# One quarter of a weight matrix on a second DMA queue, a denser request schedule and two reordered places, in a kernel of windowed attention and soft mixture of experts

## The chip, the cores and the metric

The kernel runs on one core of one Trainium2 chip. A core has a matrix engine (PE, with its weight loads shown apart as PEld), a vector engine (DVE), an activation engine (ACT), a general engine (POOL), a sync engine (SP) that only issues and waits, and sixteen DMA engines that move data between device memory and the on-chip memory. The metric is the device time of one execution in microseconds, the median over several runs.

## The reference

Eight batches of eight heads, 576 positions, 64 values a head. Each position attends to a window behind it: heads 0 to 3 to the last 32 positions, heads 4 to 7 to every fourth of the last 128. The result, 4608 rows of 512, goes through a soft mixture of experts: the rows are mixed into 32 slots (4 for each of 8 experts) by a softmax over the rows, every expert runs its 4 slots through two matrices with a ReLU between, and every row is mixed back out of the 32 slots by a softmax over the slots.

```
scores = scale * q @ k^T, masked by window; attn = softmax(scores)
x = (attn @ v) as [4608, 512]
logits = x @ phi                               # [4608, 32]
slot_input = softmax(logits over rows).T @ x
for e in range(8):                             # w1[e]: 512 x 1024, w2[e]: 1024 x 512
    slot_out[e] = relu(slot_input[e] @ w1[e]) @ w2[e]
out = softmax(logits over slots) @ slot_out
```

All inputs and the output are fp32 in device memory: q, k, v 9.4 MB each, w1 and w2 16.8 MB each, the output 9.4 MB. On the chip the kernel computes in fp16.

## The kernel before

**Transfers.** Every transfer is requested by POOL (`nc.gpsimd.dma_start`) on one queue, and the DMA turns fp32 into fp16 on the way in and fp16 into fp32 on the way out. The table of queues calls it q0. q and k of a batch come as one transfer each into the tiles `raw` (two buffers each, line 132), v as two transfers into `vs` (two buffers; line 146 the first 512 positions, line 149 the last 64, on 16 partitions). w1 of an expert is two halves, two of its four chunks of 128 rows each (line 212); w2 of experts 0 to 5 is one transfer (line 216), w2 of experts 6 and 7 is four quarters each (line 224), the columns of the first output half ahead of those of the second. An instruction of POOL that needs a buffer waits until it is free. There are eight semaphores for the transfers, used in turn, so a request also waits until the transfer eight before it has landed.

**Order.** The order on each engine is the program's own (a manual schedule). `prologue` (line 458) requests the first batch's q and k in two groups, then builds the masks, the identity and the order matrices on POOL with `affine_select` (line 483, and line 493 for `orders`), with v(0) requested between the two (line 492) and q(1), k(1), v(1) and phi behind them (lines 502 to 505). Then ten steps b = 0 to 9 run three slots each. `slot0(b)` computes the scores of the first window group, requests q and k of batch b + 2, calls `weights(b, 0)`, and carries on the batch before; `slot1(b)` computes the second group, orders v (lines 201 to 208: DVE copies `vD`, POOL copies `vL`), requests v of batch b + 2 and calls `weights(b, 1)`; `slot2(b)` computes the third group and the logits of the batch before (`back_logits`, line 397). So the work on a batch is spread over two to three steps.

**Weights.** `next_w1` (line 456) lists the sixteen halves of w1, expert by expert. `weights(b, g)` (line 520) requests one half at g = 1 of batch 0 and one at each g of batches 1 to 5, eleven in all; at batch 6 the other five, then w2 of experts 0 and 1, then w2 of expert 4 in a slab that v used. At batch 7 come experts 2, 3 and 5 and the quarters of 6 and 7, in memory that q, k and v leave free.

**ET.** `ET` (line 77, 128 partitions by 4608 + 64 columns of fp16) holds the exponentials of the logits, 576 columns a batch, written by ACT at line 409. DVE clears it whole in slot 0 of batch 0 (line 559). `back_erow` (line 411) reads columns of a batch and up to 64 columns beyond it, which the mask `emask` then multiplies by zero.

**After attention.** The slot inputs are normed, `hps` (line 670) multiplies them by w1 of all experts, and `slot_out` (line 702) multiplies the hidden values by w2, in two halves of the output columns: six experts for both halves, then experts 6 and 7 for half 0. Then `combine(0, pair)` (line 718) makes output rows 256 at a time for the columns of half 0 (two matmuls, then two ACT instructions for an even pair or one DVE instruction for an odd one, then one transfer, line 744), for eight pairs. When half 1 is there as well, `combine_full` (line 749) makes all columns of the other ten pairs, with `combine(1, ...)` of the first eight in between.

Of the kernel before, what the change touches and what calls it, by code (L numbers as in the profile page):

```python
# [44 lines left out]
NH = DMODEL // 2  # L45
# [4 lines left out]
def kernel(  # L50
# [75 lines left out]
    def load_qk(ti, b, groups=None):  # L126
        ten = (q, k)[ti]
        if (ti, b) not in raw:
            raw[(ti, b)] = raw_pool.tile([128, 2, PJ * D], FP16, name=f"raw{ti}_{b}", tag=f"raw{ti}")
        t = raw[(ti, b)]  # L130
        if groups is None:
            nc.gpsimd.dma_start(
                out=t, in_=ten[b].rearrange("(g h) (p j) d -> (h p) g (j d)", g=2, j=PJ)
            )
        else:
            for g in groups:
                nc.gpsimd.dma_start(
                    out=t[:, g, :],
                    in_=ten[b, 4 * g : 4 * g + 4].rearrange("h (p j) d -> (h p) (j d)", j=PJ),
                )  # L140

    def load_v(b):
        slab = fix.tile([128, V_SLAB], FP16, name=f"vs_{b}", tag=f"vs{b % 2}")
        sa, sb = (slab[:, 2048 * i : 2048 * i + 2048].rearrange("a (h n) -> a h n", h=H) for i in range(2))
        vstage[b] = (sa, sb)
        nc.gpsimd.dma_start(
            out=sa, in_=v[b, :, 0:512, :].rearrange("h (a r) d -> a h (r d)", r=DIL)
        )
        nc.gpsimd.dma_start(
            out=sb[0:LEFT], in_=v[b, :, 512:S, :].rearrange("h (a r) d -> a h (r d)", r=DIL)  # L150
        )
# [57 lines left out]

    def load_w1(e, i):  # L210
        src = moe_w1[e].rearrange("(c p) f -> p c f", p=128)
        nc.gpsimd.dma_start(out=w1t[e][:, 2 * i : 2 * i + 2, :], in_=src[:, 2 * i : 2 * i + 2, :])  # L212

    def load_w2(e, half=None):
        if half is None:
# [242 lines left out]
    def prologue():  # L458
        load_qk(0, 0, (0,))
        load_qk(1, 0, (0,))  # L460
        nc.vector.memset(masks, 0.0)
        nc.vector.memset(ones, 1.0)
        nc.vector.memset(orders[0:32], 1.0)
        for i in range(2):
            nc.vector.memset(kTp[i][:, S : S + 64, :], 0.0)
            nc.vector.memset(kTd[i][:, S : S + 80, :], 0.0)
            nc.vector.memset(qTd[i][:, S : S + 16, :], 0.0)
            nc.vector.memset(vP[i][:, :, :, D : D + 1], 1.0)
            nc.vector.memset(vP[i][TAIL:128, 4, :, :], 0.0)
            nc.vector.memset(vD[i][:, :, :, D : D + 1], 1.0)  # L470
            nc.vector.memset(vL[i][:, :, :, D : D + 1], 1.0)
        load_qk(0, 0, (1,))
        load_qk(1, 0, (1,))
        left = masks[:, W1:].rearrange("p (u c) -> p u c", c=LEFT)
        band = (
            (ident, ones, [[1, 128]], 0, -1, ALU.is_equal, 0.0),
            (masks[:, 0:WQ], masks[:, 0:WQ], [[1, WQ]], 0, -1, ALU.is_ge, MASKED),
            (masks[:, 0:WQ], masks[:, 0:WQ], [[-1, WQ]], WINDOW - 1, 1, ALU.is_ge, MASKED),
            (left, left, [[0, 5], [1, LEFT]], 32, -1, ALU.is_ge, MASKED),
            (left, left, [[0, 5], [-1, LEFT]], -1, 1, ALU.is_ge, MASKED),  # L480
        )
        for dst, src, pattern, base, mult, op, fill in band:
            nc.gpsimd.affine_select(  # L483
                out=dst,
                in_=src,
                pattern=pattern,
                base=base,
                channel_multiplier=mult,
                compare_op=op,
                fill=fill,  # L490
            )
        load_v(0)
        nc.gpsimd.affine_select(
            out=orders[0:32],
            in_=orders[0:32],
            pattern=[[-1, DIL], [1, 128]],
            base=0,
            channel_multiplier=-DIL,
            compare_op=ALU.is_equal,
            fill=0.0,  # L500
        )
        load_qk(0, 1)
        load_qk(1, 1)
        load_v(1)
        nc.gpsimd.dma_start(out=phi_raw, in_=moe_phi.rearrange("(p l) s -> p l s", l=4))
        nc.vector.tensor_copy(out=masks[:, WQ:W1], in_=masks[:, 0:TAIL])
        qk_plain(0, 0)
        qk_plain(1, 0)
        nc.vector.memset(emask, 1.0)
        for i in range(1, 4):  # L510
            nc.vector.tensor_copy(out=orders[32 * i : 32 * i + 32], in_=orders[0:32])
        for part in range(2):
            qk_dil(0, 0, part)
        qk_dil(1, 0, 0)
# [4 lines left out]

    def weights(b, g):  # L520
        if b < B - 2:
            if g == 1 or b > 0:
                load_w1(*next_w1.pop(0))
        elif b == B - 2:
            if g == 0:
                while next_w1:
                    load_w1(*next_w1.pop(0))
                load_w2(0)
                load_w2(1)
            else:  # L530
                slab_weights(4, "vs0", V_SLAB)
                load_w2(4)
        elif g == 0:
            raw_pool.release()
            pool = tc.alloc_tile_pool(name="w2b", bufs=1, side="right")
            late_pools.append(pool)
            for e in (2, 3):
                w2t[e] = pool.tile([128, 8, DMODEL], FP16, name=f"w2_{e}", tag=f"w2_{e}")
                load_w2(e)
        else:  # L540
            slab_weights(5, "vs1", V_SLAB)
            load_w2(5)
            slab_weights(6, "qk0", QK_SLAB)
            slab_weights(7, "v0", V_SLAB)
            for half in range(2):
                for e in HALVED:
                    load_w2(e, half)

    def slot0(b):
        att, b1, b2, b3 = b < B, b - 1 >= 0 and b <= B, 2 <= b < B + 2, b + 1 < B  # L550
        if att:
            qk_dil(1, b, 1)
            emit_scores(b, 0)
            if b + 2 < B:
                load_qk(0, b + 2)
                load_qk(1, b + 2)
            weights(b, 0)
        if b == 0:
            nc.vector.memset(ET, 0.0)
            nc.vector.memset(siTm, 0.0)  # L560
            nc.vector.tensor_reduce(
                out=halves, in_=orders[:, 0, 0:TAIL], axis=mybir.AxisListType.X, op=ALU.add
            )
            nc.vector.tensor_copy(
                out=emask[:, NE - 1, :], in_=halves.broadcast_to([128, N_SLOTS])
            )
        if b1:
            emit_av(b - 1, "d", 0)
            emit_norm(b - 1, "d", 0)
        if b2:  # L570
            back_erow(b - 2)
        if b1:
            emit_av(b - 1, "d", 1)
            emit_norm(b - 1, "d", 1)
            back_xT_plain(b - 1, 0)
        if att and b > 0:
            order_v_plain(b)
        if b == 1:
            order_phi()
        if b1:  # L580
            emit_av(b - 1, "d", 2)
            emit_norm(b - 1, "d", 2)
            back_xT_plain(b - 1, 1)
        if b2:
            back_u(b - 2)
# [129 lines left out]

    psum_f = tc.alloc_tile_pool(name="psum_f", bufs=4, space=bass.MemoryType.PSUM)

    def combine(half, pair):
        fp = psum_f.tile([128, 2, NH], FP32, name=f"f{half}_{pair}", tag="f")
        r0 = 256 * pair  # L720
        for k in range(2):
            nc.tensor.matmul(  # L722
                fp[:, k, :],
                ET[:, r0 + 128 * k : r0 + 128 * k + 128],
                so_sb[:, NH * half : NH * half + NH],
                start=True,
                stop=True,
                skip_group_check=True,
            )
        ot = out_pool.tile([128, 2, NH], FP16, name=f"ot{half}_{pair}", tag=f"ot{half}", bufs=NSPLIT // 2)  # L730
        if pair % 2 == 0:
            for k in range(2):
                blk = 2 * pair + k
                nc.scalar.activation(
                    out=ot[:, k, :], in_=fp[:, k, :], func=AF.Copy, scale=rrow[:, blk : blk + 1]
                )
        else:
            nc.vector.tensor_tensor(  # L738
                out=ot,
                in0=fp,  # L740
                in1=rrow[:, 2 * pair : 2 * pair + 2, None].broadcast_to([128, 2, NH]),
                op=ALU.mult,
            )
        nc.gpsimd.dma_start(  # L744
            out=out[r0 : r0 + 256, NH * half : NH * half + NH].rearrange("(k p) n -> p k n", k=2),
            in_=ot,
        )
# [74 lines left out]
```

## Time and profile before

| what | us |
|---|---|
| median of 11 runs | 183.22 (182.69 to 184.04) |
| the profiled execution | 183.27 |
| its span, first to last instruction | 181.6 |
| busy PE / DVE / ACT / POOL | 144.0 / 106.5 / 90.6 / 83.4 |
| first packets of q(0) / of v(0) | 2.6 / 8.7 |
| landing of k(0), second group / v(0) / q(1) / k(1) | 10.05 / 13.48 / 16.61 / 20.27 |
| a batch in steady attention | 13.6 to 13.7 |
| landing of the last w1 half | 116.05 |
| landing of w2 of expert 5 | 146.19 |
| landing of the last quarter for half 0 / of all weights | 151.53 / 156.90 |
| first output request | 153.95 |
| landing of the first and of the last output | 157.68 / 180.18 |
| granted PE clock over the span | 0.893 |

Times from the span's start unless they are lengths. A landing is the time at which the transfer's semaphore is complete. The page gives busy shares over the span and over 40 slices; the row DMA is the mean busy share of the sixteen DMA engines (a 9 is 90% or more), the row GB/s what they moved, counted where it lands: a load counts as fp16, an output as fp32. In a table by windows the last two columns are the same for a stretch of time, with the DMA share as a fraction that can exceed 1, since packets of one engine overlap. A row of the timeline has its start, its length, the engine and the line, the operation with its tiles and shapes, the count, and in brackets how long the engine had been idle and what ended that.

### The profile page before, as it was taken

The numbers are of one execution on the slowest core, as the hardware profiler recorded it, in microseconds if no ns is written. First come the engines' busy times: TensorE is split into PE (matmuls) and PEld (weight loads), VectorE is DVE, ScalarE is ACT, GpSimd is POOL, SyncE is SP. The second block draws the span as 40 slices with busy tenths as digits, with TensorE's granted clock in tenths as the row PEclk, the third lists the DMA queues.
The fourth block names the chain that finished last, engine by engine and source line by source line (L and its number), as shares of the span: only waits on it lengthen the run. The fifth ranks groups of instructions, "written<-read, shape, count | busy, mean of one in ns | idle before, by whom it ended". The sixth has DMA issues, their size and how long they took to land.

```text
span 181.6 us, 5572 instructions
## 1 busy us (share of the span) xinstructions
PE 144.0 (79%) x2464; PEld 86.6 (48%) x2464; DVE 106.5 (59%) x231; ACT 90.6 (50%) x163; POOL 83.4 (46%) x117
## 2 busy tenths in 40 slices
PE   0557987999999999999999999999879475787000
PEld 0224554656646746746746746757353263232000
DVE  4788785665884984984984984536040202499000
ACT  2053355847557667667766766764201204698000
POOL 7953642633525445445383715621101110998830
PEclk9999997898899999999999999998556968799755
DMA  4999999999999999999999999999999999999997
GB/s 64 191 170 214 197 212 202 214 208 205 210 210 205 212 210 203 211 210 203 214 208 202 212 211 211 217 214 216 217 211 217 200 195 173 307 398 410 407 408 178
DMA packets 31303, 40.75 MB, mean 224 GB/s; under 512 B 1584, under 2 KB 18992, under 8 KB 31280
## 3 DMA queue, kind: packets, MB, share of 16 engines
q0 software_dynamic: 31280, 40.41, 119.5%
q8 instruction: 19, 0.31, 0.6%
q14 instruction: 4, 0.03, 0.0%
HBM read 61.93 MB, written 9.44 MB: 393 GB/s over the span
## 4 chain that ended last, share of the span: by engine, by line
PE 43%; DMA 32%; ACT 8%; issue 5%; POOL 4%; DVE 3%; POOLq 1%
DMA w<-in_moe_w_dram 23%; PE lg L405 8%; PE o_p L336 7%; PE sa L279 6%; ACT p L290 6%; DMA raw<-in_q_dram 5%; PE sa L268 5%; PE sb L268 4%; DMA out_dram<-of 4%; PE u L447 3%; PE rd L386 2%; PE vb L162 2%; PE va L162 2%; PE rp L374 2%; ACT of L757 1%
## 5 line engine op out<-in xcount | busy, mean ns | idle before, releaser
L290 ACT ACTIVATE p<-sa 128x960 f16<-128x960 f32 (+2 forms) x24 | 21.4, 891 | 31.0 <-PE sb L279 30.4
L336 PEld LDWEIGHTS <-p 128*128 128x128 f16 (+2 forms) x544 | 19.7, 99 | 12.8 <-issue 8.6
L242 DVE STREAM_TRANSPOSE qk<-raw 128x320 uint32<-128x320 uint32 (+1 forms) x32 | 21.6, 679 | 0.3
L233 DVE STREAM_TRANSPOSE qk<-raw 128x576 uint32<-128x576 uint32 x16 | 20.0, 1252 | 2.7 <-DMA raw<-in_q_dram 1.6
L290 ACT ACTIVATE p<-sb 128x960 f16<-128x960 f32 (+2 forms) x24 | 21.2, 884 | 0.0
L208 POOL COPY v<-v 32x1024 f16<-32x1024 f16 x8 | 8.3, 1036 | 27.9 <-DVE v L201 23.0
L268 PE MATMUL sa<-masks,ident 128*128 128x480 f16 (+2 forms) x48 | 14.5, 387 | 6.2 <-POOL masks L483 4.8
L405 PE MATMUL lg<-xTd,phi 128*128 128x288 f16 x32 | 18.3, 659 | 0.0
L279 PEld LDWEIGHTS <-qk 32*128 32x128 f16 x832 | 12.3, 98 | 12.3 <-issue 8.9
L279 PE MATMUL sa<-qk 32*128 32x160 f16 (+4 forms) x416 | 16.2, 215 | 2.0 <-DVE qk L233 1.9
L336 PE MATMUL o_p<-v,p 128*128 128x65 f16 (+1 forms) x288 | 16.7, 203 | 0.8 <-ACT v L171 0.7
L224 POOL DMA_DIRECT2D w<-in_moe_w_dram x8 | 6.0, 746 | 24.3 <-DMA w<-in_moe_w_dram 24.3
L268 PEld LDWEIGHTS <-ident 128*128 128x128 f16 x96 | 9.1, 105 | 16.7 <-issue 7.1
L279 PE MATMUL sb<-qk 32*128 32x160 f16 (+4 forms) x416 | 16.3, 215 | 0.0
L358 DVE TENSOR_TENSOR xd<-o_d,rc_d 128x448 f16<-128x448 f32 (+1 forms) x24 | 14.5, 602 | 0.8
L358 DVE TENSOR_TENSOR xp<-o_p,rc_p 128x448 f16<-128x448 f32 (+1 forms) x24 | 14.5, 602 | 0.8
L744 POOL DMA_DIRECT2D out_dram<-ot x16 | 11.5, 719 | 6.7 <-PE f L722 6.7
L268 PE MATMUL sb<-masks,ident 128*128 128x480 f16 (+2 forms) x48 | 14.4, 386 | 0.2 <-ACT p L290 0.2
L212 POOL DMA_DIRECT2D w<-in_moe_w_dram x16 | 11.6, 728 | 3.1 <-DMA w<-in_moe_w_dram 2.3
L162 PE MATMUL va<-vs,orders 32*128 32x256 f16 (+1 forms) x96 | 12.1, 289 | 1.0 <-ACT p L290 1.0
L409 ACT ACTIVATE ET<-lg 128x288 f16<-128x288 f32 x16 | 6.6, 411 | 12.2 <-PE lg L405 12.1
L738 DVE TENSOR_TENSOR ot<-f,rrow 128x512 f16<-128x512 f32 x8 | 5.5, 688 | 11.9 <-PE f L722 11.8
(97 smaller groups left out, 272.0 us busy)
## 6 DMA issues: line engine op xcount, KB each, us to landing
w<-in_moe_w_dram POOLq DMA_DIRECT2D x16, 512.0 KB, 14.8
w<-in_moe_w_dram POOLq DMA_DIRECT2D x6, 1024.0 KB, 26.6
out_dram<-of POOLq DMA_DIRECT2D x10, 512.0 KB, 6.0
vs<-in_v_dram POOLq DMA_DIRECT2D x8, 512.0 KB, 10.5
out_dram<-ot POOLq DMA_DIRECT2D x16, 256.0 KB, 4.3
raw<-in_q_dram POOLq DMA_DIRECT2D x7, 576.0 KB, 13.4
raw<-in_k_dram POOLq DMA_DIRECT2D x7, 576.0 KB, 13.3
w<-in_moe_w_dram POOLq DMA_DIRECT2D x8, 256.0 KB, 23.5
```

Of the source, the lines that this page charges most:

```text
L162: nc.tensor.matmul(o.rearrange("p (h d) -> p h d", h=4), l, st[:, 0:4, D * r : D * r + D], start=(r == 0), stop=(r == DIL - 1), skip_group ...
L208: nc.gpsimd.tensor_copy(out=vL[b % NV][0:32, :, :, 0:D], in_=vD[b % NV][96:128, :, :, 0:D])
L212: nc.gpsimd.dma_start(out=w1t[e][:, 2 * i : 2 * i + 2, :], in_=src[:, 2 * i : 2 * i + 2, :])
L233: nc.vector.transpose(out=dst, in_=src)
L242: nc.vector.transpose(out=o, in_=i)
L268: nc.tensor.matmul(sps[h // 2][:, h % 2, 0:n], ident, bias[g], start=True, stop=False, skip_group_check=True,)
L279: nc.tensor.matmul(sps[h // 2][:, h % 2, c0 : c0 + w], kt_[32 * h : 32 * h + 32, k0 : k0 + 128, tt], qt_[32 * h : 32 * h + 32, q0 : q0 + w ...
L290: nc.scalar.activation(out=pt, in_=sps[ab][:, :, 0:n], func=AF.Exp, scale=SCALE)
L336: nc.tensor.matmul(o[p0 : p0 + np_, n, :], l, rr, start=(k == 0), stop=(k == len(jobs) - 1), skip_group_check=True,)
L358: nc.vector.tensor_tensor(out=x.rearrange("p t (h d) -> p (t h) d", h=4)[0:nq, u0:u1, :], in0=o[0:nq, 0:n, 0:D], in1=rc[0:nq, 0:n, None].b ...
L405: nc.tensor.matmul(lp, phi4[:, kc].rearrange("p c s -> p (c s)"), rhs, start=(kc == 0), stop=(kc == 3))
L744: nc.gpsimd.dma_start(out=out[r0 : r0 + 256, NH * half : NH * half + NH].rearrange("(k p) n -> p k n", k=2), in_=ot,)
```

## The change

1. The first quarter of w1 of expert 3 (128 rows of 1024 fp32) is left out of its half on POOL's queue. In slot 0 of batch 3, behind a DVE memset of two columns, the sync queue is given sixteen requests of 8 rows each, without conversion, into the last 2048 columns of `ET`, read as 1024 columns of fp32. In slot 0 of batch 5 POOL copies them as fp16 into the w1 tile and clears these columns of `ET`. The logits of batch 4 are the first to be written there, in slot 2 of batch 5.
2. `weights` requests one half in batch 0, three in batches 1, 3 and 5, two in batches 2 and 4, so that two are left for batch 6.
3. In the prologue v(0) is requested ahead of the selects, and q(1) ahead of the select of `orders`.
4. The first pair of output rows for half 0 is made as two blocks of 128 rows, each with its own matmul, its own ACT or DVE instruction and its own transfer.

```diff
     def load_w1(e, i):
         src = moe_w1[e].rearrange("(c p) f -> p c f", p=128)
-        nc.gpsimd.dma_start(out=w1t[e][:, 2 * i : 2 * i + 2, :], in_=src[:, 2 * i : 2 * i + 2, :])
+        c0 = 2 * i + (e == SIDE_E and i == 0)
+        nc.gpsimd.dma_start(out=w1t[e][:, c0 : 2 * i + 2, :], in_=src[:, c0 : 2 * i + 2, :])
+
+    SIDE_E, SIDE_C0 = 3, 2560
+    side = ET[:, SIDE_C0 : SIDE_C0 + 2048].bitcast(FP32)
+
+    def side_load():
+        nc.vector.memset(ET[:, SIDE_C0 : SIDE_C0 + 2], 0.0)
+        for p in range(0, 128, 8):
+            nc.sync.dma_start(out=side[p : p + 8], in_=moe_w1[SIDE_E, p : p + 8, :])
+
+    def side_cast():
+        nc.gpsimd.tensor_copy(out=w1t[SIDE_E][:, 0, :], in_=side)
+        nc.gpsimd.memset(ET[:, SIDE_C0 : SIDE_C0 + 2048], 0.0)
...
         load_qk(0, 0, (1,))
         load_qk(1, 0, (1,))
+        load_v(0)
         left = masks[:, W1:].rearrange("p (u c) -> p u c", c=LEFT)
...
-        load_v(0)
+        load_qk(0, 1)
         nc.gpsimd.affine_select(
             out=orders[0:32],
...
-        load_qk(0, 1)
         load_qk(1, 1)
...
     def weights(b, g):
         if b < B - 2:
-            if g == 1 or b > 0:
+            for _ in range((0, 1)[g] if b == 0 else (1, 1 + b % 2)[g]):
                 load_w1(*next_w1.pop(0))
...
             weights(b, 0)
+        if b == 3:
+            side_load()
+        if b == 5:
+            side_cast()
...
+    def combine_one(half, blk):
+        fp = psum_f.tile([128, NH], FP32, name=f"f{half}_one{blk}", tag="f")
+        cols = slice(NH * half, NH * half + NH)
+        r0 = 128 * blk
+        nc.tensor.matmul(fp, ET[:, r0 : r0 + 128], so_sb[:, cols], start=True, stop=True)
+        ot = out_pool.tile([128, NH], FP16, name=f"oo{half}_{blk}", tag=f"oo{half}_{blk}")
+        if blk % 2 == 0:
+            nc.scalar.activation(out=ot, in_=fp, func=AF.Copy, scale=rrow[:, blk : blk + 1])
+        else:
+            nc.vector.tensor_scalar(
+                out=ot, in0=fp, scalar1=rrow[:, blk : blk + 1], scalar2=None, op0=ALU.mult
+            )
+        nc.gpsimd.dma_start(out=out[r0 : r0 + 128, cols], in_=ot)
+
     def combine(half, pair):
+        if half == 0 and pair == 0:
+            combine_one(half, 0)
+            combine_one(half, 1)
+            return
```

## The prediction

> **What bounds the kernel.** I read the DMA row of the 40 slices and the table of queues first, since the chain of waits gives the DMA only a third and names PE most.
>
> ```profile
> DMA  4999999999999999999999999999999999999997
> GB/s 64 191 170 214 197 212 202 214 208 205 210 210 205 212 210 203 211 210 203 214 208 202 212 211 211 217 214 216 217 211 217 200 195 173 307 398 410 407 408 178
> ...
> q0 software_dynamic: 31280, 40.41, 119.5%
> q8 instruction: 19, 0.31, 0.6%
> ```
>
> From the second slice to the last the DMA engines work, at about 210 GB/s of fp16 landed (twice that read, as fp32) and then 405 GB/s of fp32 written. All kernel traffic is on queue 0; queue 8 is instruction fetch, 19 packets. Next the landings of the transfers, in order of issue: in attention a q or k of 1.18 MB read lands 2.77 us behind its forerunner, a half of w1 2.46 us, a v 2.65 + 0.36 us, and these sums fill every batch: 2 x 2.77 + 3.01 + 2 x 2.46 = 13.5 us of a batch of 13.6 to 13.7. The data lead their use: q of batches 3 to 7 lands 7.9 to 9.2 us before its transpose reads it. So PE paces attention at 13.65 us a batch, yet never lets the queue run dry, and the last weight lands when the DMA engines have done all bytes. PE waits there:
>
> ```profile
> 146.23 3.46 PE L706 MATMUL so<-w,hTm 128*32 128x256 f16 x64 [2.67 <-DMA w<-in_moe_w_dram]
> 150.18 0.29 PE L706 MATMUL so<-w,hTm 128*32 128x256 f16 x4 [0.49 <-DMA w<-in_moe_w_dram]
> 151.58 0.29 PE L706 MATMUL so<-w,hTm 128*32 128x256 f16 x4 [1.11 <-DMA w<-in_moe_w_dram]
> ...
> 156.94 0.29 PE L706 MATMUL so<-w,hTm 128*32 128x256 f16 x4 [0.47 <-DMA w<-in_moe_w_dram]
> ```
>
> These are the last weights; the last lands at 156.90, the last output at 180.18, that is 23.28 us for 9.44 MB. Now a table by windows around that handover:
>
> ```profile
> 145.00:150.00 5.00, 3.46 (x64) 2.83 (x64) 0.00 (x0) 0.00 (x0) 0.74 (x1) 0.66 1.44 195
> 150.00:152.50 2.50, 0.75 (x10) 0.45 (x10) 0.00 (x0) 0.37 (x1) 0.00 (x0) 1.00 1.45 195
> 152.50:155.00 2.50, 2.50 (x20) 1.32 (x18) 1.63 (x3) 2.19 (x6) 1.05 (x2) 0.56 0.90 125
> 155.00:157.50 2.50, 1.76 (x20) 0.76 (x13) 1.14 (x2) 1.23 (x4) 2.50 (x4) 0.75 1.70 329
> ```
>
> The last two columns are DMA share and GB/s: from 152.5 to 155 the rate drops from 195 to 125 while weights are still outstanding. Part of the engines are through, the rest are not. The semaphore records say how many: each transfer of queue 0 raises its semaphore sixteen times, once per DMA engine. For the last weights the sixteen come at 152.71 plus 0, 0.48, 0.59, 0.72, 0.80, 1.15, 1.16, 1.21 and then plus 2.34, 2.72, 3.11, 3.38, 3.47, 3.68, 4.08, 4.19. At 20 us the spread was 1.2 us but for one engine. In between it jumps by some 0.7 us for one engine after a fetch packet of queue 8 (16 KB, 0.89 to 0.97 us each); between fetches it stands still. So eight engines carry the instruction fetches and end 2.3 to 4.2 us behind, and **eight light engines** wait for output that does not exist yet. The heaviest engine never pauses from then on: its load end plus 23.28 us of output is the end of the kernel. To move the time, work must leave the heavy engines, or everything must start earlier.
>
> **The side load.** It takes one quarter of w1[3] from queue 0: 128 rows of 4 KB, eight per engine. Half a w1 is 16 rows per engine in 2.46 us, so 0.154 us a row, and each of the sixteen loses 8 x 0.154 = **1.23 us**. The sync queue brings the same rows back as sixteen requests of eight rows of fp32. Eight rows occupy at most eight engines. If they are always the same eight, each gets 16 rows. A row's price: its 4 KB read cost 0.154 us above; its 4 KB written as fp32 cost, by the outputs (512 KB in 1.25 us, 16 rows of 2 KB an engine, 0.078 each), 0.156 us. Upper bound: the 4096-byte packets of w2 (16 an engine in 4.93 us, 8 KB read each), 0.308 us. I take 0.155, the rows with the same bytes: 2.48 us per engine, 4.9 us at the upper bound. On the light eight this gives a lag of at most 1.21 - 1.23 + 2.48 = 2.46, on the heavy eight 4.19 - 1.23 = 2.96; the heaviest ends 1.23 us earlier. At the upper bound the light ones end at 4.9, 0.7 later than the heaviest now. Nothing in the trace numbers the engines, so which eight is open: I choose the light eight, and price the other two cases below.
>
> [...]
>
> The other parts of the side load are covered. The DVE memset of two columns is some 0.07 us (memset rows of that size), in slot 0 of batch 3, where DVE idles 1.51 us for ACT. The sixteen issues are SP's, which has no other work. The cast and the clearing on POOL stand behind the w1 request of batch 5:
>
> ```profile
> 82.77 0.72 POOL L212 DMA_DIRECT2D w<-in_moe_w_dram  x1
> 83.53 1.03 POOL L204 COPY v<-vs 16x1024 f16<-16x1024 f16 x1
> 88.99 1.04 POOL L208 COPY v<-v 32x1024 f16<-32x1024 f16 x1 [4.43 <-DVE v L201]
> ```
>
> A POOL copy of 1024 columns is 1.03 us; twice that for fp32 and as much for 2048 columns bounds both at 4.1 us together, and the 4.43 us wait for DVE takes it. If that cover went, the v copy, then v(7)'s request and PE's dilated units would be late in turn. DVE could lose up to the same time if it shares something with POOL; its 77% busy in these batches leaves 3 us.
>
> **Five halves instead of four.** The schedule asks for 14 w1 pieces before batch 6 instead of 11; the bytes and the order of w2 stay. Since the queue never empties, its end does not move: 0. What moves is the place of raw in the queue. Two more halves stand ahead of q(6) and q(7): 2 x 2.46 - 1.23 for the quarter taken out = 3.7 us off a lead of 7.9 us, so 4.2 us remain (the light engines, 2.48 us busier, lead by that much). POOL waits for the landing of the transfer eight before (24.3 us at line 224); a deeper queue brings that wait into attention, behind which the next raw requests stand, within the same 4.2 us.
>
> **The order of the prologue.** v(0) is requested ahead of the five selects (5.24 becomes about 3.65), q(1) about 0.65 earlier; the masks come 1.5 us later.
>
> ```profile
> 8.40:9.60 1.20, 0.99 (x24) 0.67 (x24) 1.16 (x4) 0.14 (x1) 1.20 (x2) 1.00 0.82 131
> 9.60:12.20 2.60, 1.55 (x16) 0.65 (x20) 2.50 (x5) 1.69 (x2) 1.87 (x4) 1.00 1.29 161
> 12.20:18.00 5.80, 3.94 (x78) 2.41 (x68) 4.50 (x7) 2.32 (x4) 1.85 (x3) 1.00 1.16 210
> 18.40:21.00 2.60, 2.60 (x37) 1.12 (x36) 1.51 (x4) 0.00 (x0) 2.47 (x4) 1.00 1.39 192
> ```
>
> Between the first raws and v(0) the engines starve: 131 GB/s, then 161 where the next v reaches 192. Against 200 the first window loses 1.2 x 69/200 = 0.41 us, against 192 the second 2.6 x 31/192 = 0.42. v(0) landed 3.43 us behind its forerunner instead of 2.65, which is 0.78. The first 512-byte packets appear 2.5 us after the request; 1.6 us earlier they would be there. What slows the second window the trace does not say. Bounds 0 and 0.8 us; I take **0.5 us**, for the whole queue from there on. PE's price: DVE's copy of the masks (4.74, waiting for POOL) goes to 6.2 and pushes the first transposes from 5.77 to 6.5, 0.7 us; but at 16.64 and 20.30 DVE waits 0.79 and 1.06 us for q(1) and k(1), which swallows it. If it did not, attention would end 0.7 us later and eat into the 2.67 us before 146.23.
>
> **The first output.** Its two halves go out separately: one matmul and one ACT (0.42 us) fewer before the first issue (153.95), some 0.5 us earlier, and one more POOL issue of 0.72 us. This decides nothing for the heaviest engine, which has weights left until 155.3 and needs its tenth output at about 160.6 where POOL's tenth issue is about 160 with its 1.25 us to the first packet (both less the 0.5 above). If POOL came late there, up to 0.5 us would return.
>
> **The sum**, on the profiled execution: 183.27, span 181.6 and 1.67 around it; 183.27 is 0.05 over the median 183.22. Less 1.23, less 0.5: **181.5** on the median. Its own range: prologue 0 to 0.8 and up to 0.5 back at the outputs, 181.0 to 182.4.
>
> **Rivals.** *Spread evenly* (the rows rotate over all engines, or the balance is not what ends the kernel): the side load moves nothing, the prologue alone remains, 182.7. For it: no row shows how an eight-row request is dealt out. Against: the heaviest engine's 23.28 us follow its last weight without a pause.
>
> *The eight are the heavy ones*: slower. The place is the handover at 152.5 to 157; the heaviest engine gains 1.25 us instead of losing 1.23, less 0.5: 183.22 + 1.25 - 0.5 = 184.0. It decides as soon as one engine with a lag above 4.19 + 0.5 - 1.25 = 3.44 us is among the eight; four of the heavy eight have more. For it: the trace numbers no engine. The row price of 0.308 us ends near 183.4 and is counted with it.
>
> *Attention late*: the deeper queue and POOL's waits hold back a raw or v, and the end of attention moves. PE has 2.67 us before 146.23, of which the earlier weights take 1.73; after that the waits of 0.49 and 1.11 give 1.6 more, so it decides from 2.5 us on. It needs the lead of 4.2 us to vanish first. A delay of 4.5 us would give 183.5.
>
> **Chances.** 0.64 for the forecast, 0.16 spread evenly, 0.14 heavy, 0.06 late. A measurement of this kernel tells about 0.2%, 0.37 us. Faster: the forecast and three quarters of the even case, 0.76; same: the rest of that and part of the price bound, 0.08; slower 0.16. The range reaches over the even case, 180.9 to 183.0.
>
> **What would show it.** Right: the sixteen counts of the last weights spread by some 3 us instead of 4.2, no dip to 125 GB/s, last weight near 155.2, first v within 2.8 us of its forerunner, queue of SP with 128 packets of 4096 bytes near 0.155 us an engine. Wrong: a spread of 5 us or more (heavy), an unchanged one (even), DVE waiting for raw in batches 6 and 7 or PE no longer waiting at the sixth expert (late).

## The result and the profile after

The change makes the kernel slower. The median is 185.14 us (184.76 to 186.29, 12 runs) beside 183.42 for the kernel before, a ratio of 1.0108 with a 95% interval of 1.0086 to 1.0129. The ratio is worked out from the single runs, without the slow ones, so it isn't the quotient of the two medians (1.0094). The prediction had 181.5 us and a range up to 183.0. The profiled execution took 184.96 us, its span is 183.1; before they were 183.27 and 181.6.

The page of the kernel after: granted PE clock, DMA busy share and rate in forty slices, then the queues.

```profile
PEclk9999995798589789799999999999655898899655
DMA  4999999999999999999999999999999999999996
GB/s 65 191 194 212 201 208 204 215 205 206 212 211 202 220 215 204 208 212 209 205 211 209 204 211 214 216 215 216 213 213 212 203 196 152 297 394 408 407 409 164
...
q0 software_dynamic: 31168, 40.15, 117.9%
q1 hardware_dynamic: 256, 0.52, 1.5%
q8 instruction: 19, 0.31, 0.6%
```

q1 is the sync queue, new here: 128 packets of 4096 bytes, the rows, and 128 of four bytes, eight for each request. Its 0.52 MB left queue 0 only in part: queue 0 fell from 40.41 to 40.15 MB as it counts where data land (fp16), while q1 lands fp32. Read the 1.5% as time: 0.015 x 16 engines x 183.1 us is 44 us, and the packets sum to 45.3. The GB/s row shows the loss: the low slice at the handover, 173 before, is 152 now. The table by windows around it has the columns PE, PEld, DVE, ACT and POOL busy, granted clock, DMA share and GB/s:

```profile
150.00:152.50 2.50, 0.59 (x8) 0.21 (x8) 0.00 (x0) 0.00 (x0) 0.00 (x0) 1.00 1.39 187
152.50:155.00 2.50, 1.55 (x11) 1.11 (x11) 0.59 (x2) 0.85 (x2) 0.11 (x1) 0.76 1.10 152
155.00:157.50 2.50, 2.50 (x19) 1.22 (x17) 1.87 (x3) 1.71 (x5) 2.50 (x5) 0.56 0.96 172
157.50:160.00 2.50, 1.57 (x14) 0.69 (x13) 0.96 (x2) 1.67 (x4) 2.50 (x4) 1.00 1.84 372
```

Before, one window was low (125 GB/s) and the next was back at 329. Now two are low, 152 and 172: the engines that are through wait longer for the others. PE's timeline shows that it still waits for weights to the end:

```profile
150.29 0.29 PE L723 MATMUL so<-w,hTm 128*32 128x256 f16 x4 [0.84 <-DMA w<-in_moe_w_dram]
151.64 0.29 PE L723 MATMUL so<-w,hTm 128*32 128x256 f16 x4 [1.05 <-DMA w<-in_moe_w_dram]
152.98 0.29 PE L723 MATMUL so<-w,hTm 128*32 128x256 f16 x4 [1.05 <-DMA w<-in_moe_w_dram]
...
158.33 0.29 PE L723 MATMUL so<-w,hTm 128*32 128x256 f16 x4 [0.46 <-DMA w<-in_moe_w_dram]
```

The last weight landed at 158.29 in place of 156.90, the last output at 181.60 in place of 180.18: 23.31 us behind it, 23.28 before. So all of the 1.4 us arose before the last weight. The sixteen arrivals of the last weights (the sixteen counts of the transfer's semaphore, read as one for each DMA engine), first in absolute time and then as lags behind the first:

```
before 152.71 | 0 .48 .59 .72 .80 1.15 1.16 1.21 2.34 2.72 3.11 3.38 3.47 3.68 4.08 4.19
after  151.83 | 0 .26 2.15 2.24 2.30 2.41 3.08 3.53 3.54 3.81 4.12 4.20 4.98 5.06 6.09 6.46
```

The first engine is 0.9 us earlier and the last 1.4 us later. Before there were two groups of eight; now two engines are early, twelve lie in the middle, and two stand out at the end. That is the sign which the prediction had named for its rival "heavy", a spread of 5 us or more. The rest of this study is about those two engines and about the width of the middle.

### The profile page after: what moved, and what is told of

Its sections match the earlier page's. It is cut to its first block, busy times and chain, and to the rows that moved or that the text cites. A ratio compares the mean times of both kernels' runs of the same rounds, so it can differ in the third digit from the quotient of the medians.

```text
span 183.1 us, 5612 instructions
## 1 busy us (share of the span) xinstructions
PE 146.5 (80%) x2464; PEld 87.5 (48%) x2464; DVE 106.8 (58%) x233; ACT 90.7 (50%) x162; POOL 86.0 (47%) x120
## 3 DMA queue, kind: packets, MB, share of 16 engines
q0 software_dynamic: 31168, 40.15, 117.9%
## 4 chain that ended last, share of the span: by engine, by line
PE 46%; DMA 23%; ACT 8%; issue 6%; POOL 6%; DVE 6%; POOLq 1%
DMA w<-in_moe_w_dram 20%; PE lg L418 8%; ACT p L303 7%; PE o_p L349 6%; PE sa L292 6%; PE sb L281 5%; PE sa L281 5%; PE rd L399 3%; DMA out_dram<-ot 3%; PE u L460 3%; PE vb L162 2%; PE va L162 2%; DVE qk L255 2%; PE rp L387 2%; PE o_d L349 1%
## 5 line engine op out<-in xcount | busy, mean ns | idle before, releaser
L281 PE MATMUL sa<-masks,ident 128*128 128x480 f16 (+2 forms) x48 | 15.7, 416 | 7.2 <-POOL masks L497 6.2
L281 PEld LDWEIGHTS <-ident 128*128 128x128 f16 x96 | 9.6, 112 | 18.9 <-issue 7.9
L292 PEld LDWEIGHTS <-qk 32*128 32x128 f16 x832 | 12.8, 101 | 12.0 <-issue 9.8
L292 PE MATMUL sa<-qk 32*128 32x160 f16 (+4 forms) x416 | 16.7, 219 | 0.8 <-DVE qk L246 0.7
L281 PE MATMUL sb<-masks,ident 128*128 128x480 f16 (+2 forms) x48 | 15.4, 411 | 0.5 <-ACT p L303 0.5
L370 DVE RECIPROCAL rc_p<-o_p 128x7 f32<-128x7 f32 (+1 forms) x24 | 4.7, 197 | 12.9 <-PE o_p L349 12.4
L392 ACT COPY xTp<-rp 128x576 f16<-128x576 f16 x16 | 10.4, 647 | 2.2 <-PE rp L387 2.2
```

What stands on the lines that cost most here:

```text
L281: nc.tensor.matmul(sps[h // 2][:, h % 2, 0:n], ident, bias[g], start=True, stop=False, skip_group_check=True,)
L292: nc.tensor.matmul(sps[h // 2][:, h % 2, c0 : c0 + w], kt_[32 * h : 32 * h + 32, k0 : k0 + 128, tt], qt_[32 * h : 32 * h + 32, q0 : q0 + w ...
L392: nc.scalar.copy(out=xTp_t[b][:, c, :], in_=rg)
```

## The experiments

Each kernel was timed in turn with the kernel before, on the same chip. Ratios are to the kernel before, with 95% intervals; "last weight" and the lag of the latest engine behind the first come from the profiled execution. Of each kernel one execution was profiled. Last weights that differ by some tenths of a us say little (in `halves_only` and `first_out_only` they fall 0.2 us behind that of the kernel before, with intervals that include 1), so ratios decide and arrivals explain.

| kernel | ratio | last weight | latest lag |
|---|---|---|---|
| after | 1.0108 [1.0086, 1.0129] | 158.29 | 6.46 |
| no_side | 0.9977 [0.9955, 0.9999] | 156.44 | 3.93 |
| side_only | 1.013 [1.0092, 1.0168] | 159.12 | 6.83 |
| side_whole | 0.9974 [0.9956, 0.9992] | 156.71 | 4.17 |
| own_near | 1.0083 [1.0055, 1.0112] | 159.21 | 7.20 |
| own_apart | 0.9989 [0.9967, 1.0012] | 157.02 | 5.41 |
| rows_near | 0.9997 [0.9963, 1.003] | 156.47 | 5.22 |
| rows_apart | 1.0103 [1.0057, 1.0148] | 159.41 | 7.03 |
| own_four | 0.995 [0.9931, 0.997] | 156.09 | 4.08 |
| near_four | 0.9965 [0.9946, 0.9983] | 156.17 | 4.08 |
| halves_only | 0.9984 [0.9968, 1.0001] | 157.12 | 4.47 |
| prologue_only | 0.9975 [0.9952, 0.9997] | 155.99 | 3.16 |
| first_out_only | 1.0022 [0.9995, 1.005] | 157.11 | 4.33 |
| prologue_four | 0.997 [0.9945, 0.9996] | 156.26 | 3.80 |

### no_side and side_only: which part

`no_side` is the kernel after with the quarter back on POOL's queue, and no calls of `side_load` and `side_cast`.

```diff
-        c0 = 2 * i + (e == SIDE_E and i == 0)
-        nc.gpsimd.dma_start(out=w1t[e][:, c0 : 2 * i + 2, :], in_=src[:, c0 : 2 * i + 2, :])
+        nc.gpsimd.dma_start(out=w1t[e][:, 2 * i : 2 * i + 2, :], in_=src[:, 2 * i : 2 * i + 2, :])
...
-        if b == 3:
-            side_load()
-        if b == 5:
-            side_cast()
```

> The changed kernel without the side load, its cast and its clearing; the quarter of w1 comes with its half on POOL's queue, the rest of the change stays. Theory S (the side load is the whole loss: sixteen rows cost an engine 4.1 us in place of 2.5, and two of the eight engines that get them also carry instruction fetches): last weight about 156.6 us, the sixteen arrivals of the last weight spread over about 4.2 us, ratio to the kernel before 0.998. Rival Q (the deeper queue in attention, or the later masks, cost the time): last weight near 158, ratio about 1.01.

`side_only` is the kernel before with the side load, the cast and the clearing, and nothing else of the change.

> The kernel before with the side load, its cast and its clearing, and nothing else of the change. Theory S: last weight about 158.6 us, arrivals spread over about 6.3 us, ratio 1.010 to 1.013. Rival Q: ratio 1.000 or less.

Measured 0.9977 and 1.013. The side load alone costs the whole loss; the other three parts together are faster than before by about 0.2%. In `no_side` the sixteen arrivals are two groups of eight again, lags 0 to 1.24 and 2.15 to 3.93. Its page also settles a rival: the granted clock.

```profile
PEclk9999995799589789789999999999855699579855
```

The same row of the kernel before:

```profile
PEclk9999997898899999999999999998556968799755
```

From the seventh slice to the seventeenth the row of `no_side` has nearly the digits of the kernel after, lower than before (after 57985897897, here 57995897897, before 78988999999). Attention ended later in both: the fourth w2 request, for which POOL waits until DVE has done the last transposes, came at 113.68 after and at 113.51 here, in place of 109.39. Yet `no_side` is faster than before: late attention was hidden behind the queue, and the loss isn't from there.

### side_whole: the same bytes, dealt evenly

The kernel after with one request in place of sixteen:

```diff
-        for p in range(0, 128, 8):
-            nc.sync.dma_start(out=side[p : p + 8], in_=moe_w1[SIDE_E, p : p + 8, :])
+        nc.sync.dma_start(out=side, in_=moe_w1[SIDE_E, 0:128, :])
```

> The changed kernel with the same 128 rows in one request of the sync queue, so eight rows on each of the sixteen engines. Theory S with a general price of a side row (0.255 us, as two queues share an engine): every engine pays 2.0 for the 1.23 us it saves, no engine is singled out, last weight about 157.4, ratio 1.001 to 1.004. Rival P (the high price comes from the form: one row a request, or eight neighbouring partitions): 8 x 0.155 = 1.24 us, last weight about 156.6, ratio 0.998.

Measured 0.9974: as good as no side load, with all its bytes on the sync queue. The page of this kernel:

```profile
q1 hardware_dynamic: 144, 0.52, 0.8%
```

The same 0.52 MB now take 0.8% (22.8 us summed) in place of 1.5%; beside the 128 rows there are sixteen packets of four bytes, where sixteen requests had eight each. So neither the second queue nor the bytes are dear. Dear is the manner in which sixteen requests of eight rows deal them out.

### side_apart: a confounded try

To tell the two halves of that manner apart, the requests' eight rows were set four apart, still in `ET`:

```diff
-        for p in range(0, 128, 8):
-            nc.sync.dma_start(out=side[p : p + 8], in_=moe_w1[SIDE_E, p : p + 8, :])
+        for c in range(0, 128, 32):
+            for p in range(c, c + 4):
+                nc.sync.dma_start(
+                    out=side[p : c + 32 : 4], in_=moe_w1[SIDE_E, p : c + 32 : 4, :]
+                )
```

> The changed kernel with the eight rows of each side request taken four partitions apart instead of next to one another. Rival P in its form for neighbouring partitions: a side row falls to 0.155 us, the loaded engines end some 2.5 us instead of 4.1 behind the unloaded ones, last weight about 157.2 to 157.8. Theory S: nothing changes, last weight about 158.3, ratio 1.011.

Measured 1.0137 [1.0077, 1.0196], with runs from 185.19 to 191.51 us: no answer on the side load, since something else broke. The groups of this kernel have a line that no other kernel has (operation, count, busy, mean ns, then idle time and what ended it):

```profile
L431 PE MATMUL ep<-ident,ET 32*128 32x32 f16 x40 | 2.6, 176 | 6.8 <-DMA ET<-in_moe_w_dram 6.3 <-ACT ET L425 0.4
```

PE, reading `ET` for the batch before, waited 6.3 us for the side load: with the stepped slice these transfers are held against readers of other columns. In this execution, one of the long ones (190.40 us), one batch took 23.64 us, and the DMA rate fell to 90 GB/s in one of the forty slices, from about 210. How much of this the shorter executions share no trace shows. One thing can still be used: all 128 row packets took 172 ns.

### own_near and own_apart: neighbours or not

So the side load was given a tile of its own, which needs no clearing.

```diff
-    side = ET[:, SIDE_C0 : SIDE_C0 + 2048].bitcast(FP32)
+    side = consts.tile([128, FDIM], FP32, name="side")
...
-        nc.gpsimd.memset(ET[:, SIDE_C0 : SIDE_C0 + 2048], 0.0)
```

`own_near` has this alone; `own_apart` also has the requests of `side_apart`.

> The changed kernel with a tile of its own for the side rows in place of the columns of ET, so without the clearing on POOL and without any tie between the side rows and the readers of ET; the requests are as in the change (eight neighbouring partitions). Theory S: the same as the changed kernel, last weight about 158.3 us, ratio 1.010. Rival T (the tie to ET or the clearing is part of the loss): ratio 1.005 or less.

> As own_near, with the eight partitions of a request four apart. Rival P (neighbouring partitions make a row dear): side packets near 0.17 us throughout instead of up to 0.44, the loaded engines end about 2.8 us behind the unloaded ones instead of 4.1, last weight about 157.0 to 157.8, ratio 1.003 to 1.008; the two engines with fetches among the eight still keep it above 1. Theory S without P: as own_near.

Measured 1.0083 and 0.9989. The pages, first of `own_near`:

```profile
q1 hardware_dynamic: 256, 0.52, 1.5%
```

then of `own_apart`:

```profile
q1 hardware_dynamic: 256, 0.52, 0.9%
```

The row packets took 274 ns on average in the first and 175 in the second. The difference in time, 0.0094 x 183.58 = 1.7 us, is about 16 rows x 99 ns = 1.6 us: the loaded engines take 16 rows each. In the profiled executions the last weight differs by 2.19 us. So most of the loss is that the rows of a request are neighbours.

The averages hide a pattern. In the four kernels with eight neighbours (after, `side_only`, `own_near`, `rows_apart` below) the sixteen requests ran as two bursts of eight, 1.0 to 1.4 us apart. Taken in order of time, eight packets to a request, the rows of the first two requests of the first burst took 172 ns each, those of the first of the second burst 172 to 184 on average; from the third request of a burst on the averages were 185 to 410. So a single request into neighbours was not dear here: it took several of them, one behind another.

What is left in `own_apart` shows the other half. Its arrivals:

```
own_apart 151.61 | 0 .41 2.35 2.40 2.48 2.49 2.70 2.72 2.75 2.88 3.09 3.16 3.21 3.52 4.92 5.41
```

Two, twelve, two. Eight engines carry 16 side rows, eight carry instruction fetches (2 to 4 us by the groups in `no_side`). If the two sets shared none, there would be no engine at 0 and none at 5; two at each end mean that the sets share two. This is read from counts, as the trace numbers no engine; following each lag from transfer to transfer gives the same, with the jumps after fetch packets always on one of the same eight. In `own_apart`, for one, the lag of one of the two latest went from 4.27 to 5.40 us around the fetch packet at 123.75. Fourteen engines are through at 151.61 + 3.52 = 155.13; the two that carry both end at 157.02, 1.89 us behind these. The price of a row four partitions apart comes from a transfer soon behind the side rows (it landed at 78.80): the six engines with lags of 2.40 to 3.05, loaded and not yet thrown back by fetches, stand 2.52 us behind the first two on average, which is 0.157 us for each of 16 rows.

The eight loaded engines can be seen at once in the kernel after, in the arrivals of a queue 0 transfer ahead of the side rows and of one behind them:

```
56.28 | 0 .09 .10 .17 .19 .38 .39 .53 .64 .66 .69 1.24 1.58 1.59 1.82 1.93
74.68 | 0 .24 .98 1.04 1.14 1.30 1.37 1.40 3.57 3.88 4.13 4.23 4.51 5.02 5.07 5.39
```

### rows_near and rows_apart: device memory or partitions

In all runs so far the rows of w1 in device memory and the partitions on the chip were spaced alike. These two cross them.

```diff
     # rows_near, on own_apart
-                    out=side[p : c + 32 : 4], in_=moe_w1[SIDE_E, p : c + 32 : 4, :]
+                    out=side[p : c + 32 : 4],
+                    in_=moe_w1[SIDE_E, c + 8 * (p - c) : c + 8 * (p - c) + 8, :],
     # rows_apart, on own_apart
-                    out=side[p : c + 32 : 4], in_=moe_w1[SIDE_E, p : c + 32 : 4, :]
+                    out=side[c + 8 * (p - c) : c + 8 * (p - c) + 8],
+                    in_=moe_w1[SIDE_E, p : c + 32 : 4, :],
```

> As own_apart (the whole quarter in sixteen requests of eight rows into a tile of their own, eight partitions four apart), but each request reads eight neighbouring rows of the weight in device memory; so the rows of the quarter land in another order than the reference has, and the result is that of a quarter with its rows exchanged; time and bytes are the same. Theory (neighbouring partitions on the chip are dear): packets of the sync queue at 172 ns as in own_apart, ratio near 0.999, last weight near 157.0. Rival (neighbouring rows in device memory are dear, 32 KB in one stretch read by eight engines at once): packets of 0.26 to 0.27 us as in own_near, ratio near 1.008, last weight near 159.

> The other cross: eight rows four apart in device memory into eight neighbouring partitions; the rows of the quarter are exchanged here too. Theory (neighbouring partitions on the chip are dear): packets of 0.26 to 0.27 us, ratio near 1.008, last weight near 159. Rival (neighbouring rows in device memory are dear): packets at 172 ns, ratio near 0.999, last weight near 157.0.

Measured 0.9997 and 1.0103, row packets of 175 and 282 ns. The pages, first `rows_near`, then `rows_apart`:

```profile
q1 hardware_dynamic: 256, 0.52, 0.9%
```

```profile
q1 hardware_dynamic: 256, 0.52, 1.5%
```

The price follows the partitions that are written, not the rows that are read.

### own_four and near_four: four engines

Half of the quarter (64 rows) in sixteen requests of four rows, so that only four engines should be loaded; the other 64 rows go on POOL's queue.

```diff
+        if c0 % 2:
+            nc.gpsimd.dma_start(out=w1t[e][64:128, 0, :], in_=moe_w1[e, 64:128, :])
...
-        for p in range(0, 128, 8):
-            nc.sync.dma_start(out=side[p : p + 8], in_=moe_w1[SIDE_E, p : p + 8, :])
+        for c in range(0, 64, 16):
+            for p in range(c, c + 4):
+                nc.sync.dma_start(
+                    out=side[p : c + 16 : 4], in_=moe_w1[SIDE_E, p : c + 16 : 4, :]
+                )
```

> Half of the quarter only: 64 rows on the sync queue in sixteen requests of four partitions (four apart), so sixteen rows on each of four engines; the other 64 rows come on POOL's queue. Every engine saves 0.62 us, four pay about 2.8. Theory S: if none of the four carries fetches, last weight about 155.8, ratio 0.994; with one of them among the four, last weight about 157.5 to 158.5, ratio 1.004 to 1.011. A time at 0.998 with the last weight near 156.4 would say that the last weight of the heaviest engine does not set the end.

`near_four` has four neighbouring partitions in each request (`side[p : p + 4]`).

> As own_four (64 rows of the quarter by the sync queue, sixteen requests of four partitions into a tile of their own, the other 64 rows on POOL's queue), but each request's four partitions are neighbours in place of four apart. The same bytes on the same four engines, none of which takes instruction fetches by my reading. Theory (neighbouring partitions make a side row dear: 0.26 us where four apart took 0.157): the sync queue's packets take longer than the 172 ns of own_four, the four loaded engines gain up to 16 x 0.1 = 1.6 us more; they stood near the heaviest there, so the last weight comes 0 to 1.5 us later than own_four's 156.09, ratio 0.995 to 1.003. Rival (only eight neighbours at once are dear, since eight engines then meet, or the spread comes from the fetches alone): packets near 172 ns, last weight within 0.2 us of own_four's, ratio 0.995.

Measured 0.995 and 0.9965. The arrivals:

```
own_four  152.01 | 0 .07 .08 .54 2.18 2.18 2.24 2.41 2.52 2.60 3.43 3.71 3.81 3.86 4.01 4.08
near_four 152.09 | 0 .05 .07 .54 2.04 2.25 2.71 2.75 3.05 3.19 3.35 3.41 3.45 3.47 4.00 4.08
```

Four and twelve, with no pair at the end: none of the four loaded engines carries fetches, and here the side load did no harm. q1 has 64 packets of four bytes in both, four for each request. The theory fell in `near_four`: its row packets took 192 ns on average (most 172, the longest 364) against 173 apart, not 262 to 282. Four neighbours are nearly free on average, eight are not. The excess lies almost whole in the first burst, whose requests from the fourth on took 203 to 260 on average; in the second all packets but one took 172.

### halves_only, prologue_only, first_out_only: the other parts

Each is one part of the printed diff on the kernel before: the line in `weights`; the order in `prologue`; `combine_one`.

> The kernel before with only the denser schedule (14 w1 halves before batch 6 instead of 11). Theory S: nothing, 0.998 to 1.002, last weight 156.9; q of batches 6 and 7 about 2.5 to 4.9 us closer to its use. Rival Q: slower by 0.5% or more, with DVE waiting for raw or attention ending later.

> The kernel before with part 3 of the change alone: v(0) ahead of the selects, q(1) ahead of the select of the order matrices. In the trace of after v(0) landed 2.70 us behind its forerunner in place of 3.43, and the queue stood about 0.3 us earlier at k(1). Theory (the heaviest DMA engine's bytes set the end, everything that starts earlier moves it): last weight at about 156.6, last output 0.3 us earlier, ratio 0.997 to 0.999. As I put it in the prediction: 0.5 us, 0.997. Rival (the later masks push the first transposes, and attention or a later wait swallows the gain): last weight at 156.9 or later, ratio 1.000 or above.

> The kernel before with part 4 of the change alone: the first pair of output rows of half 0 as two blocks with a transfer each. Theory: the first output request comes some 0.5 us earlier (about 153.4 in place of 153.95) and decides nothing, since the engine that ends last still has weights then: last weight at 156.9, last output 23.3 us behind it, ratio 0.998 to 1.002. Rival (one more request on POOL delays the outputs behind it, or the light engines' earlier start carries through to the end): the 23.3 us between last weight and last output change by 0.3 us or more, ratio outside 0.998 to 1.002.

Measured 0.9984, 0.9975 and 1.0022, so only the prologue differs from 1 beyond its interval, by 0.0025 x 183.41 = 0.46 us (0.06 to 0.88 by the interval). The expectation for the first output was missed by a little in size: a small loss up to 0.5% isn't excluded, and a gain beyond 0.1% is; its last output came 23.30 us behind its last weight, as before. In `halves_only` q of batches 5 to 7 led its use by 7.7, 4.3 and 4.4 us (9.1, 7.9 and 8.6 before).

### prologue_four: does a harmless side load gain?

The prologue and the side load of `own_four`, without the other two parts.

> The kernel before with part 3 (the prologue) and the side load of own_four alone: 64 rows of the quarter in sixteen requests of four partitions four apart into a tile of their own; no denser schedule, no split first output. The prologue alone gave 0.9975 with its last weight at 155.99. Theory (a side load pays where the engines that it loads carry no instruction fetches): the unloaded engines lose 4 rows each, 4 x 0.154 = 0.6 us, the loaded ones gain about 2.5 us and stay at or below the heaviest, so the last weight comes 0.3 to 0.6 us earlier than with the prologue alone, at 155.4 to 155.7, ratio 0.993 to 0.996. Rival (own_four's gain was the prologue's and the denser schedule's, the side load gives nothing): last weight at 156.0, ratio 0.9975.

Measured 0.997 [0.9945, 0.9996], last weight 156.26: the rival. Against the prologue alone (0.9975, 155.99) the side load gives nothing that these runs can see. Its first engine is 0.36 us earlier than with the prologue alone (152.46 against 152.82), but its latest lag is 0.64 us longer (3.80 against 3.16); with one profiled execution of each kernel, whether this is chance stays open. `own_four` beats both kernels (0.995), but its interval meets those of `prologue_only`, `no_side`, `side_whole`, `near_four` and `prologue_four`; which of these is best stays open. So no run shows for certain that a side load gains, even on engines without fetches.

## Why the prediction was wrong, point by point

**What ends the kernel: right.** In the traces that hold the last output it came 23.2 to 23.4 us behind the last weight, wherever that fell, but for `side_apart`, which isn't used.

**Each engine loses 1.23 us of queue 0: right, as far as two engines show.** The eight light engines before have a mean of 153.48; the two of them without side rows stand at 151.96 after, 1.52 earlier: 1.23 and some 0.3 that fit the prologue (the first eight of `prologue_only` have a mean of 153.24, 0.24 earlier).

**"If they are always the same eight, each gets 16 rows": right,** by the two-twelve-two of `own_apart` and the four-and-twelve of `own_four`. The counts agree with a fixed set; which engines these are, no run shows.

**"I choose the light eight": the first step that failed.** Six of them are light, two carry fetches as well. I had priced this as the rival "the eight are the heavy ones", at 184.0 us, and named what decides it: one engine with a late lag among the eight suffices. I gave it 0.14 because I thought of two disjoint or equal sets. In `own_apart`, where rows have the price I used, it costs 1.89 us and eats the whole gain: the other fourteen engines are through at 155.13, where the sum of the prediction (156.90 - 1.23 - 0.5) had 155.17.

**"I take 0.155, the rows with the same bytes": the second step, and the larger.** Bytes alone set the price where the partitions were apart: 0.157 us a row. In the change a row took about 0.26 us: the six loaded engines without fetches went from 153.48 to 156.1, and 2.6 + 1.23 + 0.3 over 16 rows is 0.26. Sixteen rows at 0.10 more are 1.6 to 1.7 us, about the difference of `own_near` and `own_apart` in time (1.7). So a loaded engine paid 16 x 0.26 = 4.2 us where I had 2.48. My upper bound, 0.308, held the price, but it was to end near 183.4 on its own; I didn't combine it with fetches on the same engine. Together, 155.13 + 1.89 + 2.19 = 159.21 is the last weight of `own_near`, by construction; that of the kernel after fell 0.9 us lower in its one profiled execution.

**Five halves, "0": right.** 0.9984 with 1 in its interval. The lead that I put at 4.2 us was 7.0, 6.4 and 6.5 us in the kernel after, and 4.3 at the least in `halves_only`.

**The prologue, 0.5 us: right.** 0.46 us alone, with an interval of 0.06 to 0.88. The windows of the kernel after show the hunger gone:

```profile
8.40:9.60 1.20, 0.92 (x24) 0.67 (x24) 1.17 (x4) 0.00 (x0) 1.20 (x2) 1.00 1.11 172
9.60:12.20 2.60, 1.37 (x12) 0.41 (x12) 2.49 (x6) 1.83 (x2) 1.57 (x4) 1.00 1.42 192
```

172 and 192 GB/s where it was 131 and 161; v(0) landed 2.70 us behind its forerunner in place of 3.43. DVE's copy of the masks came at 6.17, as predicted (6.2), and cost nothing that is seen.

**The first output: right.** It was requested 1.95 us behind its last weight in place of 2.42, 0.47 us sooner (0.5 predicted), and gained nothing that is seen.

**The work on POOL and DVE is covered: right.** The timeline of POOL in the kernel after:

```profile
87.06 0.72 POOL L213 DMA_DIRECT2D w<-in_moe_w_dram  x1
87.83 1.03 POOL L224 CAST w<-ET 128x1024 f16<-128x1024 f32 x1
88.92 1.80 POOL L225 MEMSET ET<- 128x2048 f16 x1
90.79 1.03 POOL L204 COPY v<-vs 16x1024 f16<-16x1024 f16 x1
93.29 1.04 POOL L208 COPY v<-v 32x1024 f16<-32x1024 f16 x1 [1.47 <-DVE v L201]
```

2.83 us for both (bound 4.1), and the wait at line 208 fell from 4.43 to 1.47, by as much. The copy of v isn't later than its cover allows. DVE's cast of v at 90.32, beside the clearing, took 0.42 us, as before at 86.02, where POOL waited.

**Attention late: it came, and was hidden; its price was wrong.** The multiplication by w1 (`hps`) began at 138.85 after and at 138.79 in `no_side`, in place of 134.71, and PE no longer waits at the sixth expert, the sign that the prediction had named. After, where the kernel before waited 2.67 us at 146.23:

```profile
146.66 2.80 PE L723 MATMUL so<-w,hTm 128*32 128x256 f16 x96 [0.39 <-DVE hTm L704]
```

The prediction let such a delay decide from 2.5 us on; in `no_side` 4.1 us cost nothing that is seen (0.9977). Its lead of 4.2 us did not have to vanish for it either, since 6.4 us were left. What set the granted clock lower in those slices no run here shows.

## What to carry to other kernels

In this kernel, whose queue is full to the end, the latest DMA engine set the end: in the traces used, the last output came 23.2 to 23.4 us behind the last weight, wherever that fell. So before moving bytes from such a queue to another, read from the sixteen arrivals of the last transfers how many engines are late, and ask of every new request how many engines and which partitions it takes. One request over all 128 partitions moved here without loss what sixteen small ones spoiled, and saved fifteen issues; it gained nothing either (0.9974, and 0.9977 without a side load). When two unknowns load the same engine, price them together: of the two here each alone leaves about the old last weight of 156.90 (fetches 157.02, measured; neighbours 155.13 + 2.19 = 157.3, worked out), and both made 1.1%.

## What the runs showed that was not expected

Requests of eight 4 KB rows into eight neighbouring partitions took 262 to 282 ns a packet on average, into partitions four apart 172 to 175, into four neighbours 192, and the first sixteen rows of the first burst 172 even into eight neighbours. Why later requests of a burst are dear, and whether the number of engines or of neighbours decides, stays open; device memory is excluded by the cross.

In these traces the instruction fetches landed on eight of the sixteen DMA engines, always the same, and a fetch left its engine about 1.1 us late to the end: in the kernel after, one engine's lag went from 5.39 to 6.43 us between the last w1 half and the first w2 (first arrivals 111.73 and 116.67) and stood there to the end. In the kernel before the eight late engines end 2.61 us behind the eight early ones on average, 1.1 us for each of 19 packets; the prediction's jump of some 0.7 us was too small. With 19 packets of 16 KB (0.31 MB, 0.6% of the engines' time) they spread the last weights over 3.2 to 4.5 us in the kernels without a side load. The four engines that took the requests of four rows in `own_four` and `near_four` were free of them.

A stepped slice of a tile as the target of a transfer held readers of other columns of that tile: 6.3 us of PE waits and a batch of 23.64 us in `side_apart`.
